# Seven block products for the output projection from the fourth chunk on, and the gate sums in another order

## The chip, the cores and the metric

The kernel runs on one core of a Trainium2 chip. The metric is the device time of one execution in microseconds; lower is better. TensorE (PE) multiplies, VectorE (DVE) and ScalarE (ACT) do the element-wise work and read TensorE's results out of PSUM, GpSimd (POOL) does a little, and SyncE (SP) issues every transfer from one queue, in order.

## The reference

A linear attention feeds a gated feed-forward layer. With batch 8, 8 heads, 576 positions and head size 64:

```
q_s = softmax(q, over head_dim);  k_s = softmax(k, over positions)
kv  = k_s^T v                      (64 x 64 per head)
x   = q_s kv                       -> 4608 tokens x 512
out = ((x @ w_a) * (x @ w_b)) @ w_out      w_a, w_b: 512 x 1536, w_out: 1536 x 512
```

All data is float32. Each operand of a matmul is written as a rounded part and a rest ("hi" and "lo"), and a product is three matmuls: hi by hi, hi by lo, lo by hi.

## The kernel before

The 4608 tokens go in nine chunks of 512 (chunk 0 to chunk 8; the fourth is chunk 3). The 1536 inner columns are twelve blocks of 128 (f), taken as six pairs (i = 0 to 5). Chunk 0 goes a plain way while the weights are still being prepared. From chunk 1 on, one pair of one chunk is a Strassen-Winograd product of a 2 x 2 block matrix of weights (`A11, A12, A22` and the sums `S1` to `S4`) with a 2 x 2 block matrix of x (`B11, B21, B22` and the sums `T1` to `T4`): seven products, each twelve matmuls of 256 columns (`product`, L689), in three PSUM banks (`kx`; `ky`, which is later `kp`; `ka`). Before, the order is A11·B11, S2·T2, S3·T3, S1·T1, A12·B21, S4·B22, A22·T4. ACT copies kx once (L1281), DVE adds the banks into `u2`, `u3` and `cc` (L1282, L1285, L1299, L1312, L1317), and four DVE products of 256 columns turn the sums into the gated values (a times b). `g_split` (L206 on ACT, L209 on DVE) splits two tiles of 512 per pair.

The projection (`project`, L710) takes a gated f, 128 x 512, as the stationary operand in four pieces of 128 tokens and w_out's rows as the moving one: twelve matmuls of 512 columns for each f, into four banks po0 to po3, which collect all twelve f of a chunk. After the last, four copies take them to SBUF (`store`, L723) and four transfers out.

Beside the products of chunk c stands the attention of chunk c + 1, dealt out in pieces by `Spread`: queries (eight exponentials of 64 columns on ACT for each of four head groups, L534), keys, their maximum, and x itself. The weights of each product are loaded from DRAM for each use (`get_w`, L335: 42 transfers of 512 KB in a chunk, eight buffers).

Up to the start of chunk 2 each engine's order is written out by hand (`ORDER`); behind that a scheduler places the instructions, engine by engine, once, when the program is built. Each engine then runs its list in order, and waits where an operand or a buffer is not ready.

## Time and profile before

| | |
|---|---|
| three runs | 959.17, 959.36, 960.6 us |
| profiled execution: first to last instruction (span) | 954.4 us |
| median of the runs less this span | 5.0 us |
| PE busy in the span | 931.9 us (98%) |
| DVE, ACT, POOL busy | 613.4, 390.6, 105.3 us |
| moved by DMA | 282.64 MB, mean 296 GB/s |

The page gives the profiled execution's span and no device time of its own; the 5.0 us between the span and the median lie around it. Busy time is the union of an engine's instructions. Matmuls overlap their neighbours, so what one costs in a dense row is the distance from start to start, not its duration.

### The profile page before, as it was taken

Reading aid. Unit: us, or ns where it says so; the run is one execution under the profiler, and the core shown is the slowest. Engines: PE = TensorE matmul, PEld = TensorE weight load, DVE = VectorE, ACT = ScalarE, POOL = GpSimd, SP = SyncE. Lnnn points to the kernel's source line nnn. Section 1 sums busy time; section 2 is a strip of 40 time slices with the busy share of each in tenths; the row PEclk is TensorE's granted clock in tenths of the full one; section 3 lists DMA queues with packets and bytes.
Section 4 is the critical chain, followed back from the end, with each engine's and each line's share of the span. In section 5 each row is a group of like instructions: output and inputs, shape, how many; then the busy total and the mean of one; then the engine's idle time right before and its main releaser. Section 6 shows DMA issues by size and latency. Waiting matters only on the chain.

```text
span 954.4 us, 17546 instructions
## 1 busy us (share of the span) xinstructions
PE 931.9 (98%) x6479; PEld 827.2 (87%) x6479; DVE 613.4 (64%) x1209; ACT 390.6 (41%) x1085; POOL 105.3 (11%) x88
## 2 busy tenths in 40 slices
PE   5999999999999999999999999999999999999998
PEld 3666667888899999999999999899999999999997
DVE  6979869677676747574756566665756556553443
ACT  7878836523363327141633244323522353121111
POOL 1555352320010001000000000000000000000000
PEclk9999999999999999999999999999999999999999
DMA  9999889898998969896899678976996779677761
GB/s 346 408 413 359 299 286 331 291 324 295 326 374 261 360 226 318 293 393 228 296 296 388 236 275 318 349 269 244 351 332 238 264 272 327 220 258 251 263 211 55
DMA packets 97588, 282.64 MB, mean 296 GB/s; under 512 B 11680, under 2 KB 12256, under 8 KB 97504
## 3 DMA queue, kind: packets, MB, share of 16 engines
q1 hardware_dynamic: 97504, 281.52, 82.9%
q8 instruction: 52, 0.85, 0.4%
q14 instruction: 32, 0.26, 0.1%
HBM read 241.40 MB, written 37.98 MB: 293 GB/s over the span
## 4 chain that ended last, share of the span: by engine, by line
PE 88%; DMA 4%; DVE 4%; ACT 1%; SPq 1%; issue 1%; POOL 0%; POOLq 0%; DVEq 0%; ACTq 0%
PE po L710 27%; PE kx L689 14%; PE kp L689 14%; PE ka L689 14%; PE ky L689 7%; PE pt L664 5%; PE po L699 3%; PE px L620 2%; PE pk L441 2%; DMA mr<-dq 2%; DMA kt_first<-in_kt 1%; DMA ws_y<-dy 1%; DVE ws L209 1%; DMA ws<-dw 1%; DVE wo_w L209 0%
## 5 line engine op out<-in xcount | busy, mean ns | idle before, releaser
L710 PE MATMUL po<-wo_w,gh 128*128 128x512 f32 x768 | 228.1, 396 | 0.0
L689 PE MATMUL kx<-xo,ws 128*128 128x256 f32 x1152 | 164.2, 284 | 0.5 <-ACT u L1281 0.3
L689 PE MATMUL ka<-xo,ws 128*128 128x256 f32 x1152 | 160.8, 282 | 2.1 <-DVE cc L1317 1.0
L710 PEld LDWEIGHTS po<-wo_w,gh 128*128 128x128 f32 x768 | 138.0, 189 | 25.7 <-ACT gh L206 0.3
L689 PE MATMUL kp<-xo,ws 128*128 128x256 f32 x1152 | 157.2, 282 | 0.0
L689 PEld LDWEIGHTS ka<-xo,ws 128*128 128x128 f32 x1152 | 149.7, 188 | 7.1 <-DVE cc L1317 1.2
L689 PEld LDWEIGHTS kx<-xo,ws 128*128 128x128 f32 x1152 | 149.7, 189 | 5.4 <-ACT qt L534 1.0
L689 PEld LDWEIGHTS kp<-xo,ws 128*128 128x128 f32 x1152 | 148.2, 188 | 4.3 <-DVE cc L1299 0.3
L710 PE MATMUL po<-wo_w,gl 128*128 128x512 f32 x384 | 137.7, 396 | 0.0
L206 ACT CAST gh<-cc 128x512 fp32r<-128x512 f32 x96 | 56.7, 620 | 143.9 <-DVE cc L1313 133.3
L1312 DVE TENSOR_TENSOR cc<-kp,u 128x512 f32<-128x512 f32 x48 | 33.1, 689 | 99.6 <-PE kp L689 99.4
L1300 ACT COPY cc<-kx 128x256 f32<-128x256 f32 x48 | 17.9, 373 | 167.0 <-PE kx L689 167.0
L710 PEld LDWEIGHTS po<-wo_w,gl 128*128 128x128 f32 x384 | 71.2, 188 | 15.8 <-DVE gl L209 0.4
L534 ACT ACTIVATE qt<-qt,st 128x64 f32<-128x64 f32 x224 | 75.3, 340 | 22.3 <-DVE st L531 14.3
L664 PE MATMUL pt<-xo,ws 128*128 128x512 f32 x288 | 83.7, 432 | 0.5 <-DVE xo L1048 0.5
L1299 DVE TENSOR_TENSOR cc<-kp,u 128x512 f32<-128x512 f32 x48 | 33.1, 690 | 74.3 <-PE kp L689 74.0
L689 PE MATMUL ky<-xo,ws 128*128 128x256 f32 x576 | 76.9, 282 | 0.8 <-DMA ws<-dw 0.7
L689 PEld LDWEIGHTS ky<-xo,ws 128*128 128x128 f32 x576 | 72.1, 188 | 2.2 <-DVE xf L806 0.9
L209 DVE TENSOR_TENSOR gl<-cc,gh 128x512 fp32r<-128x512 f32 x96 | 63.9, 685 | 13.3 <-ACT gh L206 10.7
L664 PEld LDWEIGHTS pt<-xo,ws 128*128 128x128 f32 x288 | 53.1, 189 | 22.1 <-issue 9.5
L371 POOL PARTITION_ALL_REDUCE mx<-m x20 | 18.4, 918 | 447.2 <-DVE m L382 447.2
L1281 ACT COPY u<-kx 128x512 f32<-128x512 f32 x48 | 28.0, 584 | 82.9 <-PE kx L689 82.0
(147 smaller groups left out, 1148.9 us busy)
## 6 DMA issues: line engine op xcount, KB each, us to landing
ws<-dw SPq DMA_DIRECT2D x312, 512.0 KB, 5.4
dw<-ws SPq DMA_DIRECT2D x42, 512.0 KB, 5.4
mr<-dq SPq DMA_DIRECT2D x112, 128.0 KB, 4.9
raw<-in_w_ab SPq DMA_DIRECT2D x24, 512.0 KB, 7.4
out<-ot SPq DMA_DIRECT2D x36, 256.0 KB, 4.7
vt<-in_v SPq DMA_DIRECT2D x28, 325.0 KB, 6.4
qt<-in_q SPq DMA_DIRECT2D x32, 256.0 KB, 5.2
kt<-in_k SPq DMA_DIRECT2D x24, 320.0 KB, 5.0
```

What stands on the lines that cost most here:

```text
L206: nc.scalar.copy(out=hi, in_=src)
L209: return nc.vector.tensor_tensor(out=lo, in0=src, in1=hi.bitcast(F32), op=ALU.subtract)
L441: nc.tensor.matmul(pk[h * D:(h + 1) * D], kt[:, j, h], vt[:, j, h], start=(j == 0), stop=(j == J - 1),)
L534: nc.scalar.activation(out=qt[:, j, h], in_=qt[:, j, h], func=AF.Exp, bias=st[:, h, 0, j:j + 1], accum_out=st[:, h, 1, j:j + 1],)
L620: nc.tensor.matmul(px[:, s], w, m[:, s], start=(i == 0), stop=(i == 2))
L664: nc.tensor.matmul(pt, w[:, wp], x[g][:, xp], start=(g == 0 and i == 0), stop=(g == NP - 1 and i == 2),)
L689: ins = nc.tensor.matmul(pt[:, n], w[:, n, wp, c], x[:, xp, c], start=(first and n == 0 and i == 0), stop=(i == 5), skip_group_check=True,)
L699: nc.tensor.matmul(po[t], g[:, t * P:(t + 1) * P], wo_first[f], start=(f == 0), stop=(f == NF - 1),)
L710: ins = nc.tensor.matmul(po[t], a[:, ts], wo[f][:, w], start=(f == 0 and i == 0), stop=(f == NF - 1 and i == 2),)
L1281: nc.scalar.copy(out=u2, in_=kx)
L1299: nc.vector.tensor_tensor(out=cc[:, 3], in0=kp, in1=u3, op=ALU.add)
L1312: nc.vector.tensor_tensor(out=cc[:, 1], in0=kp, in1=u2, op=ALU.add)
```

## The change

Chunks 0 to 2 keep their products and their projection. From chunk 3 on three things differ.

1. The projection of a pair is seven block products (`Q1` to `Q7`), each six matmuls of 256 columns: the gated pair is a 2 x 2 block matrix (f by halves of 256 tokens), w_out's two row blocks are another (f by halves of 256 columns). The sums on the left are made by DVE (`left_sums`, four a pair) and each of the seven left operands is split by ACT and DVE (`split_lefts`, 256 columns). The sums on the right are made once (`right_sums`, in chunk 2 and at the start of chunk 3); four of them stay in SBUF for five pairs, the others are stored to DRAM and loaded for each use (`get_right`). Q1, Q5, Q6 and Q7 all accumulate in bank po0; two pairs form a group, and after the last Q1, Q6 and Q7 (or Q5, Q7, Q6) of a group the bank is read out into or added to a tile (`snap`), while the accumulation in the bank goes on.
2. The gate products go in the order A11·B11, S1·T1, S2·T2, A12·B21, S3·T3, A22·T4, S4·B22. A11, S2, S3 and A22 accumulate one after the other in bank kx, and ACT copies the bank after each of the first three (`u3`, `u2`, `u4`; u3 and u4 share a buffer). DVE's adds fall from five to three a pair.
3. Every second chunk takes the pairs backwards, and the seven weights of a chunk's last pair stay for the next chunk's first one. From chunk 4 on the order of PE's products is fixed as written (`chained`). The last pair of chunk 8 is projected as before, at the very end.

```diff
     def get_w(i, op):
+        if (i, op) in last_w:
+            return last_w.pop((i, op))
...
+    def plan(c):
+        groups = [(0, 1), (2, 3), (4, 5)] if c < NCH - 1 else [(0, 1), (2, 3), (4,)]
...
+            text = '4a 1a 2a 6a 3a 7a 5a' if len(ps_) == 1 else '4a 2a 3a 5a 4b 2b 5b 7a 7b 3b 6a 6b 1a 1b' if back else '4a 1a 2a 3a 1b 4b 6a 6b 2b 7a 7b 3b 5a 5b'
...
+    def block_step():
...
+        pt, first = bank(c, {Q2: 1, Q3: 2, Q4: 3}.get(x.m, 0))
...
+        for t in range(2):
+            for n, (ap, wp) in enumerate(((0, 0), (0, 1), (1, 0))):
+                nc.tensor.matmul(pt[:, t], x.left[:, ap, t * P:(t + 1) * P], w[:, wp], ...)
+        if x.snap:
+            n, sign = x.snap
+            with tc.high_priority(100):
+                if sign == 0:
+                    nc.scalar.copy(out=acc_tile(c, n), in_=pt)
+                else:
+                    nc.vector.tensor_tensor(
+                        out=accs[c, n], in0=accs[c, n], in1=pt, op=ALU.subtract if sign < 0 else ALU.add
+                    )
...
+                multiply(kx, A11, B11, True)
+                with pg(100):
+                    nc.scalar.copy(out=u3, in_=kx)
+                block_step()
+                multiply(ky, S1, T1, True)
+                block_step()
+                multiply(kx, S2, T2, False)
+                with pg(100):
+                    nc.scalar.copy(out=u2, in_=kx)
+                block_step()
...
+                multiply(kz, A12, B21, True)
...
+                multiply(kx, S3, T3, False)
+                u4 = sb.tile([P, 2, H], F32, name="u3", bufs=1)
+                with pg(100):
+                    nc.scalar.copy(out=u4, in_=kx)
+                    nc.vector.tensor_tensor(out=cc[:, 3], in0=ky, in1=u4, op=ALU.add)
...
+                if not end:
+                    block_step()
+                    block_step()
...
+                multiply(kx, A22, T4, False)
...
+                last_product = multiply(ky, S4, B22, False)
```

What moves in the engines' lists is shown at three places. In the names, `ws` is a weight, `xo` a split operand (of x, or a right operand that was loaded), `kept` a right operand that stayed, `left` a split left operand, `gh` and `gl` the old split pair, `px` attention of the next chunk.

PE, chunk 3, fourth pair, from its fifth product to its last, before:

```order
L689 MATMUL kx_4704<-xo_3926,ws_4808 128x256 x12
L710 MATMUL po2_4198<-wo5_w_802,gh1_4700 128x512 x2
L710 MATMUL po2_4198<-wo5_w_802,gl1_4701 128x512
L710 MATMUL po3_4199<-wo5_w_802,gh1_4700 128x512 x2
L710 MATMUL po3_4199<-wo5_w_802,gl1_4701 128x512
L620 MATMUL px_4843<-qhl_4782,kvh1_3285 128x256 x2
L620 MATMUL px_4843<-qhl_4782,kvl1_3286 128x256
L620 MATMUL px_4843<-qhl_4782,kvh1_4475 128x256 x2
L620 MATMUL px_4843<-qhl_4782,kvl1_4476 128x256
L689 MATMUL ka_4706<-xo_3933,ws_4871 128x256 x5
L689 MATMUL kp_4793<-xo_3929,ws_4851 128x256 x12
L689 MATMUL ka_4706<-xo_3933,ws_4871 128x256 x7
```

The same pair now, from S2·T2 to its last product; the two kx rows that stand one behind the other are S3·T3 and A22·T4:

```order
L695 MATMUL kx_4906<-xo_3956,ws_4972 128x256 x12
L1403 MATMUL po0_4498<-kept10_3515,left_4414 128x256 x2
L695 MATMUL ka_4908<-xo_4018,ws_5006 128x256 x12
L1403 MATMUL po1_4521<-xo_4329,left_4415 128x256 x6
L1403 MATMUL po0_4498<-kept20_3714,left_4418 128x256 x6
L695 MATMUL kx_4906<-xo_3961,ws_5028 128x256 x12
L695 MATMUL kx_4906<-xo_4025,ws_5073 128x256 x12
L1403 MATMUL po2_4580<-xo_4329,left_4416 128x256 x6
L1403 MATMUL po3_4476<-kept31_3906,left_4414 128x256 x6
L695 MATMUL ky_4907<-xo_4021,ws_5089 128x256 x12
```

Blocks of six stand where runs of 512 columns stood, and one bank is now written by four products with three copies between them.

ACT, chunk 5, in its second pair, between two readings of kx, before (`qt` are the exponentials of the next chunk's queries, `kt` those of its keys):

```order
L1281 COPY u2_6668<-kx_6664 128x512
L206 CAST gh0_6640<-cc_6417 128x512
L206 CAST gh1_6660<-cc_6417 128x512
L534 ACTIVATE qt_6580,st_6420<-qt_6580,st_6420 128x64 x8
L534 ACTIVATE qt_6670,st_6420<-qt_6670,st_6420 128x64 x8
L406 ACTIVATE kt_6683<-kt_6683 128x640
L1300 COPY cc_6667<-kx_6664 128x256
```

And now, from the first to the third copy of kx in that pair:

```order
L1572 COPY u3_7163<-kx_7158 128x512
L540 ACTIVATE qt_7061,st_6903<-qt_7061,st_6903 128x64 x5
L1354 CAST left_4418<-cc_6900 128x256
L1354 CAST left_4419<-cc_6900 128x256
L1354 CAST left_4418<-cc_6900 128x256
L1578 COPY u2_7162<-kx_7158 128x512
L1443 COPY acc_7254<-po0_5958 128x512
L540 ACTIVATE qt_7164,st_6903<-qt_7164,st_6903 128x64 x6
L1354 CAST left_4419<-cc_6900 128x256
L540 ACTIVATE qt_7164,st_6903<-qt_7164,st_6903 128x64 x2
L412 ACTIVATE kt_7177<-kt_7177 128x640
L1594 COPY u3_7332<-kx_7158 128x512
```

The exponentials now lie between copies that the next product in kx needs.

PE, the last rows of the program, before:

```order
L710 MATMUL po0_9977<-wo11_w_1425,gh1_10733 128x512 x2
L710 MATMUL po0_9977<-wo11_w_1425,gl1_10734 128x512
L710 MATMUL po1_9978<-wo11_w_1425,gh1_10733 128x512 x2
L710 MATMUL po1_9978<-wo11_w_1425,gl1_10734 128x512
L710 MATMUL po2_9979<-wo11_w_1425,gh1_10733 128x512 x2
L710 MATMUL po2_9979<-wo11_w_1425,gl1_10734 128x512
L710 MATMUL po3_9980<-wo11_w_1425,gh1_10733 128x512 x2
L710 MATMUL po3_9980<-wo11_w_1425,gl1_10734 128x512
```

And now (`pl` are the banks of the plain last pair):

```order
L1654 MATMUL pl_12017<-xo_11918,xo_11958 128x512 x2
L1654 MATMUL pl_12017<-xo_11918,xo_11959 128x512
L1654 MATMUL pl_12017<-xo_11920,xo_11938 128x512 x2
L1403 MATMUL po0_11197<-kept11_3518,left_4419 128x256 x6
L1654 MATMUL pl_12017<-xo_11920,xo_11939 128x512
L1403 MATMUL po0_11197<-kept10_3515,left_4419 128x256 x6
```

The last two block products, Q7 and Q5 of the fifth pair, stand at the very end, in the bank that is read out between them and after them.

## Rows read from the trace of the kernel before

**Rows 1.** The page: its first line, and part 1's line of busy time (us, share of the span, instructions).

```profile
span 954.4 us, 17546 instructions
...
PE 931.9 (98%) x6479; PEld 827.2 (87%) x6479; DVE 613.4 (64%) x1209; ACT 390.6 (41%) x1085; POOL 105.3 (11%) x88
```

**Rows 2.** Busy time by stretch, about one chunk each: the stretch and its length; busy us (and instructions) of PE, PEld, DVE, ACT, POOL; PE's granted clock; share and rate of the DMA engines.

```profile
240.00:340.00 100.00, 97.91 (x728) 90.71 (x727) 67.78 (x139) 39.01 (x115) 3.45 (x4) 0.98 0.91 322
340.00:440.00 100.00, 100.00 (x760) 93.02 (x759) 63.35 (x132) 36.83 (x111) 3.72 (x4) 1.00 0.83 301
440.00:540.00 100.00, 100.00 (x759) 93.16 (x758) 63.26 (x132) 36.85 (x112) 3.73 (x4) 1.00 0.86 302
...
640.00:740.00 100.00, 100.00 (x753) 93.00 (x753) 62.84 (x131) 36.83 (x111) 3.73 (x4) 1.00 0.83 293
740.00:848.00 108.00, 108.00 (x740) 100.03 (x739) 60.62 (x115) 37.81 (x114) 0.00 (x0) 1.00 0.79 269
848.00:954.00 106.00, 102.59 (x699) 94.19 (x697) 42.55 (x74) 16.75 (x32) 0.00 (x0) 1.00 0.59 203
```

**Rows 3.** Everything that PE waited for from 345 us to the end: us in total, times, longest.

```profile
PE ky L689 <- DMA ws<-dw: 0.7, 1, 0.7
```

**Rows 4.** PE in order of time in chunk 4: start, duration, what. Two gate products of twelve matmuls, the first and the last of a run of twelve projection matmuls (three, one, one, one, two, one, two, one), and the product behind it.

```profile
524.11 1.60 PE L689 MATMUL ky<-xo,ws 128*128 128x256 f32 x12
525.55 1.60 PE L689 MATMUL ka<-xo,ws 128*128 128x256 f32 x12
526.99 0.86 PE L710 MATMUL po<-wo_w,gh 128*128 128x512 f32 x3
...
529.56 0.39 PE L710 MATMUL po<-wo_w,gl 128*128 128x512 f32 x1
529.79 1.35 PE L689 MATMUL kx<-xo,ws 128*128 128x256 f32 x10
```

**Rows 5.** Groups of equal instructions with their shapes: count, busy us and mean ns, idle time before them and what ended it. DVE's subtraction and ACT's cast of a split, DVE's add from PSUM, ACT's copies of a bank and of half a bank, DVE's product and its subtraction at 256 columns.

```profile
L209 DVE TENSOR_TENSOR gl<-cc,gh 128x512 fp32r<-128x512 f32 x96 | 63.9, 685 | 13.3 <-ACT gh L206 10.7 <-PE po L710 2.7
L206 ACT CAST gh<-cc 128x512 fp32r<-128x512 f32 x96 | 56.7, 620 | 143.9 <-DVE cc L1313 133.3 <-PE ky L689 5.6 <-DVE cc L1318 3.1
L1299 DVE TENSOR_TENSOR cc<-kp,u 128x512 f32<-128x512 f32 x48 | 33.1, 690 | 74.3 <-PE kp L689 74.0
...
L1281 ACT COPY u<-kx 128x512 f32<-128x512 f32 x48 | 28.0, 584 | 82.9 <-PE kx L689 82.0 <-DVE st L538 0.9
...
L1300 ACT COPY cc<-kx 128x256 f32<-128x256 f32 x48 | 17.9, 373 | 167.0 <-PE kx L689 167.0
...
L209 DVE TENSOR_TENSOR kvl<-kv,kvh 128x256 fp32r<-128x256 f32 x10 | 4.2, 421 | 0.2
```

**Rows 6.** All engines in order of time in chunk 5: four DVE instructions in a row, and the end of a product in kx with ACT's copy of it.

```profile
586.49 0.69 DVE L1312 TENSOR_TENSOR cc<-kp,u 128x512 f32<-128x512 f32 x1 [1.02 <-PE kp L689]
...
587.09 0.68 DVE L1317 TENSOR_TENSOR cc<-ka,u 128x512 f32<-128x512 f32 x1
587.69 0.42 DVE L1313 TENSOR_TENSOR cc<-cc 128x256 f32<-128x256 f32 x1
...
588.02 0.42 DVE L1318 TENSOR_TENSOR cc<-cc 128x256 f32<-128x256 f32 x1
...
589.11 0.50 PE L689 MATMUL kx<-xo,ws 128*128 128x256 f32 x2
...
589.45 1.58 PE L689 MATMUL ky<-xo,ws 128*128 128x256 f32 x12
589.65 0.59 ACT L1281 COPY u<-kx 128x512 f32<-128x512 f32 x1 [0.37 <-PE kx L689]
```

**Rows 7.** ACT in order of time in chunk 5: the second and the last of eight exponentials of queries in a row, and one of keys.

```profile
560.05 0.33 ACT L534 ACTIVATE qt<-qt,st 128x64 f32<-128x64 f32 x1
...
562.04 0.33 ACT L534 ACTIVATE qt<-qt,st 128x64 f32<-128x64 f32 x1
...
562.48 0.74 ACT L406 ACTIVATE kt<-kt 128x640 f32<-128x640 f32 x1
```

**Rows 8.** Transfers from 340 to 440 us: GB/s in 40 slices, the amount, and a weight's load with KB each and median us from issue to landing.

```profile
GB/s 313 380 354 8 310 110 206 356 365 161 273 295 364 296 319 383 410 406 417 269 337 191 205 185 212 374 382 411 412 403 417 416 415 391 340 293 220 82 336 23
DMA packets 10306, 30.10 MB, mean 301 GB/s; under 512 B 1264, under 2 KB 1328, under 8 KB 10297
...
ws<-dw SPq DMA_DIRECT2D x42, 512.0 KB, 5.9
```

**Rows 9.** The last 11 us in order of time: the last split's cast, the two matmuls that waited for the split, the last matmul and the last copy.

```profile
943.81 1.24 ACT L206 CAST gh<-cc 128x512 fp32r<-128x512 f32 x2 [8.64 <-DVE cc L1313]
...
944.48 0.74 PE L710 MATMUL po<-wo_w,gh 128*128 128x512 f32 x2
945.21 0.19 PEld L710 LDWEIGHTS po<-wo_w,gl 128*128 128x128 f32 x1 [0.43 <-DVE gl L209]
...
950.20 0.40 PE L710 MATMUL po<-wo_w,gl 128*128 128x512 f32 x1
950.63 0.59 ACT L723 COPY ot<-po 128x512 f32<-128x512 f32 x1 [0.81 <-PE po L710]
```

**Rows 10.** The smallest transfer from the list of all transfers: KB and us from issue to landing.

```profile
ident<-in_eye SPq DMA_DIRECT2D x1, 64.0 KB, 2.0
```

More of the change, by code (lines that the diff above doesn't have):

```diff
@@ L1315, in linear_attention_then_gated_ffn @@
[L1315 to L1320 removed]
+                if c == BY_BLOCKS - 1 and p > 0:
+                    right_sums(p - 1)
+                if po is None and not blocks_of:
+                    po = [ps.tile([P, DM], F32, name=f"po{t}") for t in range(TT)]
```

364 lines of the change are left out of this document (317 added, 47 removed).

## The prediction

> **What bounds the kernel now.** The page's busy times come first: PE works 931.9 of the span's 954.4 us, DVE 613.4, ACT 390.6 [rows 1]. The windows of one chunk each show that this is no mere average: from 340 to 740 us PE is busy in every microsecond, at a granted clock of 1.00, the 2.4 GHz level; DVE has 63 of 100 us, ACT 37, and the DMA engines 0.83 to 0.86 of their time [rows 2]. Third, PE's waits: from 345 us to the end the list gives one wait of 0.7 us [rows 3]. So PE's columns set the time, and each microsecond less on PE counts as long as no other engine hands its part over late. The base of the sum is the profiled execution: span 954.4 + 5.0 around it = 959.4 us, beside a median of 959.36.
>
> **PE, the gain.** What a matmul costs in a dense row is read from start to start. Twelve gate matmuls of 256 columns take 525.55 - 524.11 = 1.44 us, 0.12 each; twelve projection matmuls of 512 columns take 529.79 - 526.99 = 2.80 us, 0.2333 each [rows 4]. The projection of a pair was 24 of the latter, 5.60 us; it becomes 7 x 6 = 42 of 256 columns, in the shape of the gate products, 42 x 0.12 = 5.04 us. The gate products stay 84 a pair in either order. That is 0.56 us a pair, and 6 chunks x 6 pairs less the last, plain one make 35 pairs: **-19.6 us**.
>
> The Trainium skill (TensorE: Matmul & The Clock Gate, "Wait — 56ns, not 53.3ns?") gives N / 2.4 GHz + about 2.5 ns a matmul, as an estimate 109 and 216 ns here, so 35 x 0.59 = 20.7 us. The rows show 120 and 233 ns; they decide, and 19.6 stays.
>
> **DVE and ACT, the load.** In a dense stretch DVE starts a 512-column instruction every 0.60 us and a 256-column one every 0.34 [rows 6], less than their durations of 0.685 and 0.421 [rows 5]. A pair was 5 adds + 2 splits of 512 columns and 4 products of 256: 7 x 0.60 + 4 x 0.34 = 5.56 us. Now it is 3 adds of 512, and 4 products, 4 left sums and 7 split rests of 256: 3 x 0.60 + 15 x 0.34 = 6.90. Six snaps and five final sums of 512 come to each chunk, 6.6 us. Together 6 x 1.34 + 6.6 = +14.7 us, from 63 to some 77 of 96 us a chunk. ACT had a copy of a bank (0.584), one of half a bank (0.373) and two casts (0.620) a pair [rows 5], with pitches a little below these some 2.1 us; now three copies and seven casts of 256 columns. For such a cast, not in the rows, I take 0.30 us, half of 0.620, between nothing and the 0.373 of the half bank: 3.8 us. With the stores' copies replaced by three snaps and one copy that is +10 to +12 us, from 37 to about 48 of 96. Both have room on average: no term by itself, unless a single stretch is full.
>
> **Hand-overs in kx.** The bank is now written by A11, S2, S3 and A22, with a copy of ACT after each of the first three. What PE must wait if nothing stood between two of them is read from chunk 5: the next product starts at 589.45, 0.16 before the old one's last group ends at 589.61; ACT starts at 589.65 (+0.04) and takes 0.59 [rows 6]; a matmul starts 0.05 after what it waited for, as at the end, where the first of two casts is over at 943.81 + 0.62 = 944.43 and its matmul starts at 944.48 [rows 9]. So 0.16 + 0.04 + 0.59 + 0.05 = 0.84 us. One block product (0.72 us) hides all but 0.12, two (1.44 us) all of it. In the fixed order two blocks, or a product of 1.44 us, stand at each place, so from chunk 4 on I cost these copies at nothing where ACT is free; the cover is gone where ACT is busy or the order differs:
>
> - *Chunk 3*, ordered by the scheduler. The change's first list shows A22·T4 directly behind S3·T3 in its fourth pair; the second and sixth go the same way: 3 x 0.84 = 2.5. One pair with a single block before A12 and one with two snaps close together add 1.5: **+4.0** (0 to 6).
> - *The second pair of chunks 4 to 7.* From the first pair's A12 add to the second's, DVE has 11 instructions of 512 and 17 of 256 columns: 6.6 + 5.8 = 12.4 us, and the attention's, of which a chunk has 63 - 6 x 5.56 = 30 us, a sixth 5 [rows 2, 6]: 17.4 us of work in a PE period of 96.2 / 6 = 16.0. If DVE comes late, u4 (in u3's buffer) cannot be copied, and A22 waits on PE. ACT's list agrees: between the copies to u2 and u4 now stand eight exponentials at 0.33 from start to start (2.66 us), a copy, a cast, and one of keys of 0.74 [rows 7]: 4.2 us, where PE has some 6 us of work. The full 1.4 us excess is one bound, with slack left from the pair before 0 the other, 2.5 with a late ACT too. I take 1.0 a chunk: **+4.0** (0 to 10).
>
> **The end.** The last pair of chunk 8 is plain and S3, A22 stand with no block between: 0.84. The last two blocks, Q7 and Q5, use one bank that DVE reads between them: 0.16 + 0.04 + 0.69 [rows 5] + 0.05, less one 512-column matmul between (0.23) = 0.70. Before, PE waited 0.29 + 0.43 here for the split [rows 9]; the plain pair still does. After the last matmul came a copy and a store of 256 KB, to the span's end 954.4 - 950.6 = 3.8 us [rows 9]. Now a copy (0.6), an add (0.6), and three or four half-bank sums (1.4) precede the store of a half (128 KB; between 2.0 for 64 KB [rows 10] and 3.2, I take 2.6): 5.3 less 3.8 is 1.5 more, less what can overlap. Sum **+2.3** (0 to 4).
>
> **Transfers.** Chunk 2 stores right operands, 6.0 MB, chunk 3 loads 22 x 256 KB and stores 0.75 MB, later chunks load 5.8 MB of them and save 7 x 512 KB = 3.7 MB of weights. The densest slices move 415 GB/s [rows 8], so these cost 14.5, 15.7 and 5 us of the engines' time. On shares of 0.91, 0.83 and 0.83 to 0.86 [rows 2] chunk 2 gets to 105 us of work in 100, chunk 3 to 98 in 96, later chunks to 88 in 96. Eight buffers hold a lead of 8 x 2 = 16 us over a landing of 5.9 [rows 8], so a short excess is borrowed from it. I take **+1** (0 to 7).
>
> Sum: 959.4 - 19.6 + 4.0 + 4.0 + 2.3 + 1.0 = **951.1 us**, own range 946 to 956.
>
> **The rivals.**
>
> *A. All cover holds.* Neither chunk 3 nor the second pairs stall: 959.4 - 19.6 + 2.3 = 942 (941 to 946). For it: DVE at 77 and ACT at 48 of 96, and slack that carries over. Against it: the two bare neighbours in chunk 3's list, which no other engine can cover. Chance 0.20.
>
> *B. The one-bank hand-overs show in every pair; slower.* The same 0.84 us, or a snap in po0 (four of the seven blocks write it), comes out each time because ACT reaches its copy late behind exponentials and casts in its list. From (19.6 - 2.3) / 35 = 0.49 us a pair nothing is gained; at 0.84 it is 959.4 - 19.6 + 2.3 + 29.4 = 971.5 us. For it: ACT's list above and a bank count that leaves kx one bank. Against it: 1.44 us of other matmuls stand in the gap in chunks 4 to 8, and ACT's average load is half. Chance 0.14. This is the side on which the Trainium skill stands (Perfetto Trace Analysis, "Matmuls"): independent matmul groups should rotate through different banks so that reading one overlaps the next group, and larger matmuls are more efficient than small ones. Rows 4 bear out its second half, 0.120 against 2 x 0.1167 for double the columns, 3%; the first no row before can show.
>
> *C. Transfers bind in chunks 2 and 3.* PE waits for weights or right operands for the whole excess, 7 us in place of 1, and some stay behind later: 951 + 7 = 958 (956 to 961). For it: 105 us in 100. Against it: PE's only wait for a weight was 0.7 us [rows 3], at shares of 0.83 to 0.91. Chance 0.11.
>
> *D. The columns are not saved.* A block's matmul would take 0.133 us or more, and 42 cost the old 5.60; with the 11 us of losses 970. The gate products have just this shape at 0.120 [rows 4]. Chance 0.02.
>
> **How the numbers follow.** My forecast has 0.53, A 0.20, B 0.14, C 0.11, D 0.02. 0.2%, 1.9 us, is about what a measurement of this kernel can tell from no change, so faster means below 957.4: forecast, A, and 0.05 of C give 0.78; same is the rest of C, 0.06; slower, over 961.3, is B and D, 0.16. The range must leave out at most 0.20: B and D above (0.16) and the lowest part of A (0.04). That gives 942 to 960.
>
> **What would show it.** Starts of block matmuls 0.12 us apart, 35 x 42 = 1,470 of them; a chunk from the fifth on takes about 96 to 97 us where it took 99.6; DVE has some 77 us of it and ACT 48. PE's waits from chunk 3 on, one line before, should name the kx copies of u2 and u4 and snaps, some 10 us in all, concentrated in chunk 3 and the second pairs; below 4 us A is right, above 17 us, spread over all pairs, B, and waits for weights or right operands of over 5 us C. At the end PE should stop about 5 us before the span does. The forecast is wrong if DVE's pitch in the new small instructions is well above 0.34 us (at 0.42, 35 x 15 x 0.08 = 42 us more work fill its slack and every pair stalls), or if the waits in kx are paid in no list that I read.

## The result, and the profile after

The changed kernel takes 968.17 us in the median (963.97 to 970.25, 7 runs); the kernel before takes 959.36 (956.47 to 961.8, 7 runs beside it). The ratio is 1.0076, 95% interval 1.0051 to 1.0101: about 7 us slower, where 8 us faster had been forecast and 942 to 960 given as the range.

The page of the changed kernel, first line and busy times, answers to [rows 1]:

```profile
span 966.1 us, 19712 instructions
...
PE 920.6 (95%) x7109; PEld 846.4 (88%) x7109; DVE 722.1 (75%) x1572; ACT 484.4 (50%) x1346; POOL 102.9 (11%) x88
```

PE's work fell by 11.3 us, but it is no longer dense. The windows, with the columns of [rows 2], show where:

```profile
240.00:340.00 100.00, 95.67 (x704) 87.31 (x703) 77.91 (x163) 41.64 (x119) 3.25 (x4) 1.00 0.98 351
340.00:440.00 100.00, 95.57 (x797) 91.30 (x796) 75.17 (x173) 50.15 (x147) 3.26 (x4) 1.00 0.99 361
440.00:540.00 100.00, 95.95 (x837) 93.59 (x837) 77.37 (x184) 51.34 (x154) 3.52 (x4) 1.00 0.92 303
...
640.00:740.00 100.00, 98.25 (x861) 96.39 (x860) 76.93 (x183) 51.23 (x153) 4.12 (x4) 1.00 0.95 316
740.00:848.00 108.00, 105.53 (x874) 104.46 (x873) 79.88 (x178) 52.20 (x159) 0.00 (x0) 1.00 0.90 316
```

From 340 us on every window of PE has a hole of 2 to 4 us where there was none, at a granted clock of 1.00 as before. DVE's 77 and ACT's 51 us are near the forecast (77 and 48 of 96). The DMA engines are busy 0.98 and 0.99 of the two windows that hold most of chunks 2 and 3, and 0.90 to 0.95 of the later ones, near what the sum had given (88 of 96). PE's longest waits from 345 us to the end, which had been one line of 0.7 us [rows 3]; the whole list adds up to 14.8:

```profile
PE kx L695 <- ACT u L1594: 4.6, 6, 1.5
PE kx L695 <- DMA ws<-dw: 2.8, 2, 1.7
PE px L626 <- DVE xf L812: 2.0, 2, 1.1
PE kx L695 <- ACT u L1578: 1.4, 1, 1.4
PE pk L447 <- DVE sst L553: 1.0, 2, 0.6
```

L1594 is the copy to u4 behind S3·T3, the one that A22·T4 needs. The bare hand-over stands in chunk 3 as the order had shown it; here in its sixth pair, PE in order of time (start, duration, and in brackets the idle time before it):

```profile
455.97 1.58 PE L695 MATMUL kx<-xo,ws 128*128 128x256 f32 x12
458.27 1.70 PE L695 MATMUL kx<-xo,ws 128*128 128x256 f32 x12 [0.73 <-ACT u L1594]
```

From start to start 2.30 us pass where twelve matmuls take 1.43: 0.87 us for a forecast 0.84. (The 0.73 in the brackets is counted from the modelled end of the last matmul, and so is less.)

The longest u4 wait has another cause. All engines in chunk 4, in its fourth pair:

```profile
518.76 3.89 SPq L581 DMA_DIRECT2D mr<-dq  x4
...
523.39 0.69 DVE L587 TENSOR_TENSOR qtt<-qtt,mr 128x512 f32<-128x512 f32 x1 [3.73 <-DMA mr<-dq]
...
524.00 0.68 DVE L1587 TENSOR_TENSOR cc<-ka,u 128x512 f32<-128x512 f32 x1
...
524.77 0.58 ACT L1594 COPY u<-kx 128x512 f32<-128x512 f32 x1
...
525.41 1.68 PE L695 MATMUL kx<-xo,ws 128*128 128x256 f32 x12 [1.48 <-ACT u L1594]
```

`mr` are rows of the next chunk's softmax (maxima and denominators), stored to DRAM (`dq`) and loaded back spread over 64 partitions, 16 transfers of 128 KB a chunk. They land late, DVE stands for 3.73 us at the instruction that needs them, the gate sum L1587 stands behind it, u4 shares the buffer that L1587 frees, and A22 waits on PE. Summed from 355 to 960 us, DVE's waits for these rows are, in the kernel before and in the changed one (line, releaser: us, times, longest):

```profile
DVE qtt L581 <- DMA mr<-dq: 1.7, 1, 1.7
```

```profile
DVE qtt L587 <- DMA mr<-dq: 15.3, 8, 4.0
```

The issues of transfers from 459 to 855 us show it too, the rows most of all: KB each and median us from issue to landing, changed kernel first, the kernel before (its second profile, e4 below) behind it.

```profile
ws<-dw SPq DMA_DIRECT2D x140, 512.0 KB, 6.7
mr<-dq SPq DMA_DIRECT2D x64, 128.0 KB, 7.8
dq<-sst SPq DMA_DIRECT2D x4, 32.0 KB, 6.2
```

```profile
ws<-dw SPq DMA_DIRECT2D x168, 512.0 KB, 5.2
mr<-dq SPq DMA_DIRECT2D x64, 128.0 KB, 4.7
dq<-sst SPq DMA_DIRECT2D x4, 32.0 KB, 2.2
```

The end, which answers to [rows 9]: Q7's accumulation is read, Q5 waits for it, and after the last matmuls (958.21 on) DVE has a row of sums.

```profile
957.47 0.69 DVE L1415 TENSOR_TENSOR acc<-acc,po 128x512 f32<-128x512 f32 x1 [2.78 <-PE po L1403]
...
958.21 0.98 PE L1403 MATMUL po<-kept,left 128*128 128x256 f32 x6 [0.55 <-DVE acc L1415]
...
959.23 0.58 ACT L1443 COPY acc<-po 128x512 f32<-128x512 f32 x1 [8.98 <-PE po L1403]
...
961.50 1.42 DVE L1661 TENSOR_TENSOR acc<-pl,acc 128x256 f32<-128x256 f32 x4
```

**By chunk.** A chunk is taken from the first matmul of its first product to the next chunk's (504 product matmuls each), chunk 8 to the span's end. "Columns" is what its matmuls take at the pitches of their shapes (0.119 and 0.232 us for 256 and 512 columns), the rest are waits and, in chunk 8, the end behind the last matmul. Lengths in us, of one profile each; e1, e3, e7 and e13 are experiments below.

| chunk | before (e4) | columns | after | columns | e1 | e3 | e7 | e13 |
|---|---|---|---|---|---|---|---|---|
| 1 | 110.5 | 98.6 | 110.3 | 98.5 | 110.7 | 110.4 | 110.0 | 113.2 |
| 2 | 104.2 | 99.7 | 106.6 | 99.6 | 104.6 | 108.6 | 105.0 | 105.4 |
| 3 | 99.4 | 98.6 | 102.2 | 93.6 | 97.9 | 105.7 | 97.5 | 102.3 |
| 4 | 99.6 | 98.9 | 101.8 | 95.4 | 99.8 | 94.7 | 98.4 | 98.4 |
| 5 | 99.9 | 99.2 | 100.7 | 95.8 | 98.6 | 101.5 | 98.1 | 99.5 |
| 6 | 100.2 | 99.5 | 100.7 | 96.1 | 98.9 | 98.2 | 97.4 | 98.8 |
| 7 | 96.4 | 96.2 | 95.5 | 92.8 | 95.5 | 94.6 | 93.2 | 92.6 |
| 8 | 103.2 | 98.7 | 106.2 | 97.5 | 106.5 | 104.1 | 104.5 | 106.2 |

The columns of chunks 3 to 8 add to 591.1 before and 571.2 after: 19.9 us were saved, as forecast (19.6). The lengths of these chunks, less columns and less the end behind the last matmul's start (4.2 us before, 7.2 after), leave 3.4 us of waits before and 28.7 after. So waits took back 25.3 us, the end 3.0, and chunk 2 another 2.4.

### The profile page after: what moved, and what is told of

The parts are those of the page before. It is cut to its first block, busy times and chain, and to the rows that moved or that the text cites. A ratio compares the mean times of both kernels' runs of the same rounds, so it can differ in the third digit from the quotient of the medians.

```text
span 966.1 us, 19712 instructions
## 1 busy us (share of the span) xinstructions
PE 920.6 (95%) x7109; PEld 846.4 (88%) x7109; DVE 722.1 (75%) x1572; ACT 484.4 (50%) x1346; POOL 102.9 (11%) x88
## 4 chain that ended last, share of the span: by engine, by line
PE 71%; DMA 16%; DVE 6%; SPq 3%; ACT 2%; issue 1%; DVEq 0%; ACTq 0%
PE kx L695 19%; PE po L1403 13%; PE ky L695 10%; PE pt L670 7%; PE ka L695 6%; DMA ws<-dw 6%; PE po L716 5%; PE po L705 4%; DMA xo<-dr 2%; PE kp L695 2%; DMA kt<-in_k 2%; PE pk L447 2%; DMA mr<-dq 2%; DMA qtt<-in_q_late 2%; SPq L581 2%; PE px L626 1%
## 5 line engine op out<-in xcount | busy, mean ns | idle before, releaser
L695 PE MATMUL kx<-xo,ws 128*128 128x256 f32 x2016 | 272.1, 284 | 12.4 <-ACT u L1594 4.6
L695 PEld LDWEIGHTS kx<-xo,ws 128*128 128x128 f32 x2016 | 252.2, 188 | 19.4 <-ACT u L1594 6.0
L1354 ACT CAST left<-cc 128x256 fp32r<-128x256 f32 x245 | 93.3, 405 | 112.6 <-DVE cc L1588 33.2
L1355 DVE TENSOR_TENSOR left<-cc,left 128x256 fp32r<-128x256 f32 x245 | 97.7, 419 | 29.4 <-ACT left L1354 28.9
L1403 PE MATMUL po<-kept,left 128*128 128x256 f32 x720 | 106.4, 283 | 1.4 <-DVE left L1355 0.9
L1403 PE MATMUL po<-xo,left 128*128 128x256 f32 x750 | 106.7, 282 | 0.2 <-DVE acc L1415 0.2
L695 PE MATMUL ka<-xo,ws 128*128 128x256 f32 x720 | 97.0, 282 | 1.9 <-DMA ws<-dw 1.1
L1403 PEld LDWEIGHTS po<-xo,left 128*128 128x128 f32 x750 | 96.6, 189 | 0.6 <-DVE acc L1415 0.4
L1403 PEld LDWEIGHTS po<-kept,left 128*128 128x128 f32 x720 | 94.5, 189 | 2.4 <-DVE left L1355 1.1
L716 PE MATMUL po<-wo_w,gh 128*128 128x512 f32 x192 | 55.3, 398 | 0.6 <-ACT gh L208 0.6
L1587 DVE TENSOR_TENSOR cc<-ka,u 128x512 f32<-128x512 f32 x36 | 24.8, 689 | 33.8 <-PE ka L695 33.3
```

Source lines behind the costliest of these rows:

```text
L695: ins = nc.tensor.matmul(pt[:, n], w[:, n, wp, c], x[:, xp, c], start=(first and n == 0 and i == 0), stop=(i == 5), skip_group_check=True,)
L716: ins = nc.tensor.matmul(po[t], a[:, ts], wo[f][:, w], start=(f == 0 and i == 0), stop=(f == NF - 1 and i == 2),)
L1354: nc.scalar.copy(out=a[:, 0], in_=cc[:, n, part])
L1355: nc.vector.tensor_tensor(out=a[:, 1], in0=cc[:, n, part], in1=a[:, 0].bitcast(F32), op=ALU.subtract)
L1403: nc.tensor.matmul(pt[:, t], x.left[:, ap, t * P:(t + 1) * P], w[:, wp], start=(first and t == 0 and n == 0), stop=(n == 2), skip_group_ch ...
L1587: nc.vector.tensor_tensor(out=cc[:, 0], in0=kz, in1=u3, op=ALU.add)
```

## The experiments

Each was run beside the kernel before on the same chip; ratios are to it, and at 959 us 0.001 is about 1 us. The changed kernel's ratio is 1.0076. An edit does more than its lines say: the scheduler places every program anew, and in chunk 3 nothing holds PE's order. In the changed kernel S3·T3 and A22·T4 stand bare, one behind the other, in three pairs of chunk 3; so they do in e13, but in e1 and e6 in one pair only. And one profile is no exact measure of a chunk: in e11 all engines have the same instructions in the same order as the changed kernel from chunk 3 to 7, and yet its chunks 4 to 7 are 5.3 us shorter (393.4 for 398.7).

**e1: the loads of right operands left out** (changed kernel).

```diff
         w = moved[x] = held["ring"][n % 4 // 2][:, n % 2]
-        nc.sync.dma_start(out=w.bitcast(F32), in_=d_right[x.i, x.m])
+        if n < 4:
+            nc.sync.dma_start(out=w.bitcast(F32), in_=d_right[x.i, x.m])
```

> Leaves out all loads of right operands after the first four (121 of 125 transfers of 256 KB); the block products read whatever lies in the ring, so only the time counts. Theory T (transfers): the new loads keep the transfer engines at 0.93 to 0.98 of their time, other loads land late, and DVE, ACT and PE wait for them in their order; then this kernel is 6 us or more below the changed one (under 962), and PE's waits for weights (6 us in the profile of after) and the late u4 copies of the fourth pairs go. Theory H (hand-overs and order): the loss is PE's waits for copies of kx, the cut-up keys' products and the longer end, which no load causes; then it stays within 3 us of the changed kernel (965 to 970).

Measured: 957.29 us, ratio 0.9992 (0.9964 to 1.0020). Leaving out the loads wins 0.0084, some 8 us (4 to 12 by the two intervals), as the first theory had it, and PE waits for no weight from 345 us on. But of the 10.0 us that chunks 3 to 8 get shorter in the profiles 4.3 lie in chunk 3, where two of the three bare hand-overs go with the new placing. And the rows stay late: DVE waits 10.2 us for them (15.3), and they land in a median 7.5 us (7.8), so their lateness is not the loads' doing alone. Without the loads the kernel is still no faster than before: as much again went elsewhere.

**e2: the new order of the gate products alone**, in the kernel before (old projection, no chain).

```diff
+            if c < 3:
                 multiply(kx, A11, B11, True)
...
+            else:
+                kz = ka
+                multiply(kx, A11, B11, True)
...
+                multiply(ky, S1, T1, True)
+                multiply(kx, S2, T2, False)
...
```

> The kernel before with the new order of the gate products and their adds from chunk 3 on, the old projection, all else old. Theory H: the one-bank order costs PE a wait for a copy of kx in many pairs, some 0.1 to 0.2 us a pair and more beside the attention: 962 to 968. Theory T: DVE and ACT have less to do and no transfer is added, so it is within 2 us of the kernel before (957 to 961).

Measured: 973.73 us, ratio 1.0163 (1.0119 to 1.0206), more than either theory gave. PE waits from 355 us on:

```profile
PE ka L689 <- DMA ws<-dw: 5.1, 7, 2.0
PE kx L689 <- DMA ws<-dw: 2.1, 3, 1.0
PE kx L689 <- DVE cc L1359: 1.8, 1, 1.8
PE kx L689 <- ACT u L1343: 1.7, 5, 0.7
...
PE kx L689 <- ACT u L1330: 0.7, 1, 0.7
```

No transfer was added here, and yet weights come late. So the order is a loss by itself, if the scheduler is to place it; only a part of it is the copies of kx. Why the weights are late here is not shown. The keys' products still stand in 8 runs of 40.

**e3: the block products alone**, in the old order of the gate products, without the fixed order.

```diff
-            held["chain"] = (c, p) >= (4, 0)
+            held["chain"] = False
...
-            if c < BY_BLOCKS:
+            if True:
                 multiply(kx, A11, B11, True)
...
```

> The changed kernel with the old order of the gate products (banks kx, ky, ka in turn, five adds a pair) and PE's order left to the scheduler in all chunks; block products, right operands and the reversed turns stay. Theory T: the loads are all there, so it is no better than 964. Theory H: the hand-overs of kx are gone and the keys' products stand together, so most of the 19.6 us of saved columns shows: 950 to 957, less what the busier DVE takes.

Measured: 958.65 us, ratio 1.0002 (0.9982 to 1.0022), between the two forecasts: 7 us better than the changed kernel and level with the one before. In this run DVE waits for no row at all from 355 us on, with the same loads. Chunks 4 and 7 show what the blocks give (94.7 and 94.6 us), chunks 2 and 3 take 10.7 back.

The longest of PE's waits in chunk 3 costs more than its own 4.0 us. DVE is held up by the attention's work in its list, and behind the wait TensorE's granted clock is at the lower of its two levels (1.2 GHz for 2.4). Two rows of PE, and the window from 402.0 to 405.4 us with its granted clock of 0.51:

```profile
401.32 2.37 PE L695 MATMUL kp<-xo,ws 128*128 128x256 f32 x12 [4.00 <-DVE u L1512]
403.49 1.48 PE L1403 MATMUL po<-xo,left 128*128 128x256 f32 x6
402.00:405.40 3.40, 3.40 (x18) 3.40 (x17) 1.97 (x5) 0.97 (x2) 0.00 (x0) 0.51 0.80 274
```

From start to start the twelve take 2.17 us instead of 1.43.

**e4: the kernel before once more.**

> The kernel before once more, for a second profile of it. Both theories: ratio 1.000 with an interval of about 0.002 on either side; if its profile is of a run near 959 us, the places where it is longer than the first profile (a run of some 956.4) show what of the 4 us that chunks 1 and 2 seem to have lost is a difference between runs.

Measured: 958.59 us, ratio 1.0005 (0.9981 to 1.0028). Its profiled run took 956.46 with a span of 954.7, so 1.8 us lie around a span, not the 5.0 that I had put in: by that, the profile of before was of a run some 3 us faster than the median. Its chunk 1 is 110.5 us (108.3 in the first profile), with PE waiting 2.6 for weights; in the profiles of all kernels here chunk 1 takes from 108.3 to 113.5 us.

**e5: the attention's matmuls in the fixed order too** (changed kernel).

```diff
+                begin = len(traced)
                 for now in self.todo[:want]:
                     for s in now:
                         s()
+                if held.get("chain"):
+                    chained.extend(x for x in traced[begin:] if x.engine == mybir.EngineType.PE)
```

> The changed kernel with the attention's matmuls put into the fixed order of PE too, where they are written: from chunk 4 on the 40 matmuls of a pair of keys' products stand together again (8 runs where 22 were from 340 us on). Theory K (cut-up keys): each extra run of them costs PE some 0.35 us (22 runs took 19.2 us, before 8 took 12.0), and with it go 4 to 6 us: 962 to 964. Theory D (late DVE and ACT, through transfers and the second pairs' load): the cut pieces only fill time in which PE would wait anyway, and it stays within 2 us of the changed kernel (966 to 970), with longer waits for u4.

Measured: 996.45 us, ratio 1.0389 (1.0361 to 1.0418). PE's longest waits from 459 to 890 us:

```profile
PE pst L551 <- DVE st L545: 18.4, 4, 4.9
PE po L1406 <- DMA xo<-dr: 4.4, 4, 1.4
```

Keys' products stand together, and PE pays with a wait of 4.6 us a chunk for the softmax sums. So theory K fails as a cure: where they are written, the attention's results are not ready. What a cut-up run costs is not tested by it.

**e6: the right operands' loads with a quarter of the bytes.**

```diff
-        nc.sync.dma_start(out=w.bitcast(F32), in_=d_right[x.i, x.m])
+        part = P if n < 4 else 32
+        nc.sync.dma_start(out=w.bitcast(F32)[0:part], in_=d_right[x.i, x.m][0:part])
```

> The changed kernel with as many transfers of right operands as now, each with a quarter of its bytes from the fifth on (32 of 128 partitions, 64 KB); the rest of an operand is whatever lies in the ring, so only the time counts. If the bytes are what costs (theory B), it is within 3 us of the kernel without the loads (957 to 960). If the number of issues and their place in SP's queue are what costs (theory Q: each waits in the one queue for its ring slot, and weights stand behind), it stays at 964 to 969.

Measured: 965.59 us, ratio 1.0067 (1.0040 to 1.0094). Three quarters of the bytes are gone, and by the ratio 0.0009 is won, within intervals that allow up to 4 us. So the bytes are not shown to be what the loads cost, nor ruled out as a part of it. The profiled run, the fastest of five (962.54 us), has chunks 3 to 8 4.5 us shorter than the changed kernel's, but 2.7 of it in chunk 3, where two bare hand-overs go as in e1.

**e7: e3 without the loads** (the edit of e1 in e3).

> Block products with the old order of the gate products (as e3) and no loads of right operands after the first four (as e1); the operands are wrong, only the time counts. If loads and the new order are the two losses and add up, it is some 10 us below e3 and e1 both: 946 to 951. If DVE's extra work is a loss of its own (77 of 96 us), it stays above 953, with PE's waits for DVE in many pairs.

Measured: 953.36 us, ratio 0.9933 (0.9914 to 0.9952), the only one clearly below the kernel before, though by 6.4 us and not by the 19.6 of its columns, and above the 946 to 951 expected. The other reading, DVE's work as a loss of its own, lacks its sign: from 345 us on PE waits 4.9 us in all, 2.9 of it for DVE, in a few places and not in many pairs. Against e3 the loads cost 0.0069, 6.6 us (4 to 9); against e1 the new order with its chain costs 0.0059, 5.7 us (2 to 9), where no load is in the way. So in a table of two by two, loads and order each cost about as much with the other as without. The ten runs go with the granted clock: 947.95 us, the profiled one, at a mean of 0.999; 949.71 and 950.36 at 0.997; 954.11 and 956.25 at 0.992.

**e8: the fixed order from the third pair of chunk 3.**

```diff
-            held["chain"] = (c, p) >= (4, 0)
+            held["chain"] = (c, p) >= (3, 2)
```

> The changed kernel with the fixed order of gate and block products from the third pair of chunk 3 on instead of from chunk 4. Theory H for chunk 3: the two bare hand-overs of S3 to A22 there (0.89 us each) and what stands around them go: 1.5 to 3 us less, 965 to 966.5. Rival: the scheduler had put them so because something else was late; then chunk 3 stays at 102 us.

Measured: 969.20 us, ratio 1.0103 (1.0078 to 1.0128). Neither forecast came: chunk 3 is longer, 105.2 us. Two of the three u4 waits go, and waits for the attention come in their place (px 2.9, pst 1.2).

**e9: the right operands' loads in POOL's queue.**

```diff
-        nc.sync.dma_start(out=w.bitcast(F32), in_=d_right[x.i, x.m])
+        nc.gpsimd.dma_start(out=w.bitcast(F32), in_=d_right[x.i, x.m])
```

> The changed kernel with the right operands' loads issued by POOL, in a queue of their own, instead of SP; same bytes, same ring. Theory Q (SP's one queue): the loads wait there for a slot of the ring (64.8 us of SP's time from 355 to 850 us in the profile of after), and weights, queries and broadcast rows stand behind them and land late; then most of the 11 us that the loads cost goes: 957 to 962. Theory B (bytes and busy transfer engines): the bytes are the same, so 965 to 970. If POOL's own issuing is slow, its blocks wait and it is above 970.

Measured: 978.17 us, ratio 1.0208 (1.0174 to 1.0242), some 13 us more than the changed kernel. DVE still waits 15.9 us for rows, so in this run SP's waiting for the ring is not what makes them late. It is no clean test, since POOL itself now waits (456 us for PE in front of these issues), with the keys' maxima behind.

**e10: e3 with the loads in POOL's queue.**

> Block products with the old order of the gate products (as e3), the loads of right operands in POOL's queue (as e9). Theory Q: near the kernel without those loads (e7, 953.4): 951 to 956, faster than the kernel before. Theory B: as e3, 957 to 960.

Measured: 962.90 us, ratio 1.0043 (1.0024 to 1.0063): above both forecasts, and worse than e3 by 4 us.

**e11: the last blocks ahead of the plain pair.**

```diff
-    behind_each_other(chained)
     for engine, names in ORDER.items():
...
                         )
+                        chained.append(ins.ins)
...
+    behind_each_other(chained)
```

> The changed kernel with the last block products ahead of the plain pair's matmuls on PE, in a fixed order; nothing else. From the last matmul's start to the span's end 7.2 us pass in after (4.2 before), and Q7 to Q5 has a wait of 0.71. Both theories: the snap, the copy and the sums of the last group come under the plain pair's matmuls (11 us), so the end takes 4 to 4.5 us and the wait goes: 2.5 to 3.7 us less than after, 964.5 to 966. If DVE's order at the end is what counts, the end stays over 6 us.

Measured: 967.36 us, ratio 1.0104 (1.0039 to 1.0168), too wide to tell by the time. The profile, of a run of 960.34 us, tells: from the last matmul's start to the end 4.1 us (7.2), while the blocks' own waits for snaps rise from 0.71 to 1.75; chunk 8 is 1.9 us shorter.

**e12: e3 with the end of e11.**

> Block products with the old order of the gate products (as e3) and the last block products ahead of the plain pair's matmuls (as e11). In e3 6.3 us lie between the last matmul's start and the span's end, in e11 4.1. If the end is a loss of its own, it is 2 to 2.5 us below e3 in the same terms: ratio 0.997 to 0.999, 956 to 958. If the last group's sums only move their wait to the front of the plain pair, it stays at 1.000.

Measured: 959.34 us, ratio 0.9992 (0.9978 to 1.0007): with e3 at 1.0002, a gain of 1 us, within the intervals. Level with the kernel before.

**e13: the rows loaded once and used again.**

```diff
+    rows_kept = {}
...
-                box["r"] = q_rows(c, g, every["dq"])
+                if c < 5:
+                    box["r"] = rows_kept[g] = q_rows(c, g, every["dq"])
+                else:
+                    box["r"] = rows_kept[g]
```

> The changed kernel in which the broadcast rows of the queries (16 transfers of 128 KB a chunk) are loaded for chunks 3 and 4 alone and used again in all later ones, which leaves out their loads from chunk 5's on; the values are wrong, only the time counts. Theory M (late rows): DVE's waits for them (15 us in after) go, and with them the stalls of PE in the fourth pairs: 4 to 7 us less than after, 961 to 964. Theory B (bytes): 2 MB a chunk less, by the 2.6 us that e6 gave for 4.3 MB some 1 us: 966 to 968.

Measured: 960.06 us, ratio 1.0010 (1.0000 to 1.0020): 6.3 us less than the changed kernel (4 to 9), for 2 MB a chunk, while e6 got no clear gain for 4.3 MB. All that PE waited for from 459 to 855 us is then

```profile
PE kx L695 <- ACT u L1599: 0.9, 2, 0.7
PE pk L447 <- DVE sst L553: 0.6, 1, 0.6
PE pk L447 <- issue: 0.4, 1, 0.4
```

No wait for a weight is left either, though all loads are there, and chunk 7 takes 92.6 us, what its columns take (92.8). Theory M held: in chunks 4 to 7 PE's listed waits are 8.6 us in the changed kernel, 3.8 without the loads (e1) and 1.2 without the rows. There rows and loads cost together, in the stretch in which the rows go through SP's list. The edit takes away the rows' 64 transfers from 459 to 855 us, their bytes and DVE's standing for them at once, and does not say which counts.

**e14: the rows first in SP's list.**

```diff
...
-                nc.sync.dma_start(
...
+                with tc.high_priority(300 if roomy(c) else 0):
+                    nc.sync.dma_start(
...
```

> The changed kernel with a higher priority for the broadcast rows and for the store they read, so that in SP's list all 16 stand together where the first stood, ahead of the weights and right operands that stood among them; all bytes stay. Theory M: DVE's waits for the rows fall from 15 to under 5 us, and the kernel gains 2 to 5 us on after: 963 to 966. If the weights behind them come late instead, PE's waits for weights rise by as much: 967 to 970.

Measured: 966.82 us, ratio 1.0089 (1.0063 to 1.0114): no gain. DVE waits for no row any more, but PE waits for what stands behind them (459 to 855 us):

```profile
PE ky L697 <- DMA ws<-dw: 5.7, 2, 3.4
PE pst L551 <- DVE st L545: 1.6, 1, 1.6
PE po L1405 <- DMA xo<-dr: 1.3, 2, 0.9
```

By this profile the lateness is moved, not removed. It is of the slowest of four runs (972.37 us; the other three took 965.09 to 967.26), and behind its waits of 3.41 and 2.28 us for weights the granted clock falls to 0.50 from 518.4 and from 723.2 us.

**e15: e14 with the end of e11.**

> The rows first (as e14) and the last block products ahead of the plain pair (as e11). If the two losses are separate, their gains add: 960 to 964, at best even with the kernel before. If it is no better than e14, the end costs nothing by itself.

Measured: 965.23 us, ratio 1.0067 (1.0043 to 1.0091); 2 us better than e14, within the intervals.

**e16 and e17: the rows in half as many transfers**, in the changed kernel and in e12.

```diff
...
+                    nc.sync.dma_start(
+                        out=rows[w],
+                        in_=dq[g, :, w].unsqueeze(1).broadcast_to([2, D, T]),
+                    )
...
```

> The changed kernel with the broadcast rows of chunks 4 to 8 in 8 transfers of 256 KB where there were 16 of 128 KB, same bytes and values. Theory N (number in flight): SP's waits for landings fall from 90 us to some 60 and DVE's waits for rows from 15 to under 8; the kernel gains 2 to 5 us on after: 963 to 966. Theory B (bytes): no gain over 1 us, 967 to 969.

> Block products in the old order of the gate products, the last blocks ahead of the plain pair (as e12), and the rows merged (as e16). Theory N: the waits for weights and right operands in the fourth pairs (some 3 us in e12) shrink: 955 to 958, ratio 0.996 to 0.998, faster than the kernel before. Theory B: as e12, 0.999 to 1.000.

Measured: 1125.26 and 1118.99 us, ratios 1.1738 (1.1705 to 1.1771) and 1.1673 (1.1644 to 1.1701). Each chunk with such rows takes some 30 us more. Transfers from 459 to 855 us, GB/s in 40 slices:

```profile
GB/s 258 336 286 183 293 396 407 253 96 49 94 200 233 378 359 125 164 344 386 403 372 116 97 51 139 279 260 392 300 106 241 323 389 380 145 49 94 94 262 275
```

Two or three slices of a chunk, of 10 us each, move 49 to 97 GB/s, while PE waits up to 16.4 us for the load of a right operand. One such stretch, in the columns of [rows 2]:

```profile
550.00:560.00 10.00, 2.00 (x9) 2.00 (x10) 2.44 (x6) 2.67 (x7) 0.00 (x0) 0.57 0.13 49
```

The DMA engines are busy 0.13 of the time, the work of about two of the sixteen, so they are not full; a transfer of this form is slow, and the loads behind it come late. Part of the 30 us is the clock: behind the waits it stands at 0.50 for up to 30.7 us at a stretch (from 438.8 us). On the number of transfers the two say nothing.

**e18: one transfer of 512 KB for two of the right operands.**

```diff
-        nc.sync.dma_start(out=w.bitcast(F32), in_=d_right[x.i, x.m])
+        if n < 4:
+            nc.sync.dma_start(out=w.bitcast(F32), in_=d_right[x.i, x.m])
+        elif n % 2 == 1:
+            two = held["ring"][n % 4 // 2].bitcast(F32)
+            nc.sync.dma_start(out=two.rearrange("p a b c -> p (a b c)"), in_=d_right[0, "whole"].rearrange("p a b -> p (a b)"))
```

> The changed kernel with one transfer of 512 KB for every two of 256 KB of the right operands, from the fifth on; it fills the same ring with other data, so only the time counts. Same bytes, half the number, in packets of 4 KB where they were 2 KB. Theory N: about half of what leaving them out gave (11 us): 961 to 965, SP's waits for landings under 65 us. Theory B: within 2 us of after (966 to 970), less what the larger packets save (some 1 us).

Measured: 972.59 us, ratio 1.0148 (1.0120 to 1.0176), worse by 7 us. Half the number does not help; each transfer now needs two free slots of the ring, and SP's longest wait for PE in front of one is 6.8 us. Theory N fails in this form.

## Why the prediction was wrong

**What held.** The pitch of a block matmul (0.119) and the 19.6 us of columns (19.9). The bare hand-over (0.84 us forecast, 0.87 to 0.89), Q7 to Q5 (0.70, measured 0.71). Chunk 3's hand-overs (4.0 forecast; u4 2.7 and u2 1.6 there). DVE's load. ACT's is a little more than worked out, because a cast of 256 columns takes 0.405 us and not the 0.30 that I had taken, which is above even the bound of 0.373:

```profile
L1354 ACT CAST left<-cc 128x256 fp32r<-128x256 f32 x245 | 93.3, 405 | 112.6 <-DVE cc L1588 33.2
```

**What came out near for another reason.** For the second pairs of chunks 4 to 7 I had forecast 1.0 us each, as A22 waiting for a late copy to u4. About their fifth product the list names 0.56, 0.22, 0.47 and 0.73 us. But only the 0.22, in chunk 5, is A22 behind that copy. In chunks 4 and 6 a keys' product waits for DVE's copy of the softmax sums (L553), and in chunk 7 the transposes of these sums (pst) wait for the copy; there DVE had stood 1.5 us for a query's load. The size is partly luck.

**The step that failed** is the transfers' term: "so a short excess is borrowed from it. I take **+1** (0 to 7)". The loads cost 8 us (e1 against the changed kernel, 4 to 12; 6.6 in the old order, e7 against e3), where I had taken 1; that is above the upper bound of 7 too, though by less than the intervals can tell. I had added bytes at the rate of the densest slices and looked at the weights' lead. What I left out is what else goes through SP's list: the softmax rows, which go out to DRAM and come back, and for which DVE stands in front of the gate sums. In the changed kernel DVE waits 15.3 us for them, and in chunks 4 to 7 PE's listed waits fall from 8.6 us to 1.2 without the rows (e13, all loads in place) and to 3.8 without the loads (e1, all rows in place). So there the price is rows and loads together. The rows had no place in the sum. It is not the whole of the loads' price: in the old order DVE waits for no row (e3), and yet the loads cost 6.6; in the two profiles most of it, 8.2, lies in chunk 3 (e3 less e7), where PE's order differs between the two. Rival C, with 7 us in chunks 2 and 3, was the nearest in size; but its sign, over 5 us of waits for weights or right operands, did not come (2.8).

**The second failure** is a term that the sum did not have: what the fixed order does to the attention's matmuls. "From chunk 4 on I cost these copies at nothing where ACT is free" looks at the copies alone. The new order with its chain costs 5.7 us without any loads (e1 against e7), no more than the 8.0 that I had put in for hand-overs, but it is made up otherwise. Around fixed products the attention falls into the gaps that are left. The keys' products stood in 8 runs of 40 from 340 us on, now in 22. In the kernel before, and in the changed one:

```profile
567.80 1.39 PE L441 MATMUL pk<-vt,kt 128*64 128x65 f32 x40
569.12 1.57 PE L689 MATMUL kp<-xo,ws 128*128 128x256 f32 x11
```

```profile
575.42 0.33 PE L447 MATMUL pk<-vt,kt 128*64 128x65 f32 x2
575.67 1.57 PE L695 MATMUL kx<-xo,ws 128*128 128x256 f32 x11
```

From the start of the matmul before a run to the start of the one behind it, less the 0.119 us of the former, a run of 40 takes 1.41 us and one of two 0.35. All runs together take 11.3 us before and 16.5 in the changed kernel, with 1.0 of waits for the softmax sums in it: 5.2 us that stand nowhere in the sum. Between e7 (12 runs) and e1 (20) they go from 12.2 to 16.5. The rows point to the chain rather than the order as what cuts them: chunk 3, in the new order without the chain, holds them in 3 runs, the chained chunks 4 to 6 in 5, 8 and 6; and e2, the order without blocks or chain, leaves them whole. In e13 chunks 4 to 6 still hold 2.7 to 3.7 us beyond their columns, where the kernel before has 0.7; keys' runs and the waits in front of them are most of the difference. On the Trainium skill's rule (Perfetto Trace Analysis, "Matmuls": rotate independent groups through banks), the trace agrees where two products stand bare, 0.87 us each, as far as the rule applies: these products add up in one bank and are independent only in what is read between them. But that is a small part of what the order costs, and e2, where PE's listed waits for copies are 2.4 us in all, loses 15.6.

**The smaller ones.** After the last matmul the end took 3.0 us more, for 1.5: DVE's sums do not overlap, they stand in one row. Chunk 2, for which only the transfers' term spoke, grew by 2.4 us in these two profiles; in those of e1, e5, e6, e8, e9, e11, e13 and e14, which share it, it takes 104.4 to 106.6 us, 104.2 and 104.7 before, so about 1 us is the change's. And the 5.0 us around the span were 2, the rest a difference between runs: against profiles alone the miss is 966.1 for 946.1.

**The sum.** In profiles, before (e4) to after: -19.9 columns, +25.3 waits in chunks 3 to 8, +3.0 at the end, +2.4 in chunk 2 and +0.5 ahead of it give +11.3; the spans differ by 11.4. Of the waits some 10 go with the loads (e1's chunks 3 to 8 are that much shorter, the new placing of chunk 3 included), and 5.2 are the longer keys' runs.

**What stays open.** How a load of 256 KB hurts is not shown. Its bytes (e6) won nothing clear, half its number (e18) won nothing, though each transfer then needs two slots, and taking it out of SP's list (e9) did not bring the rows in time, though that run put POOL in the way. DVE's waits for the rows follow neither the loads nor the order alone: 15.3 us in the new order with the loads and 10.2 without (e1), 0 in the old order with the loads (e3) and 7.3 without (e7). So the order in which SP issues them, dq's store and weights between them, may have a part; e14, which changed that order, won nothing clear. What each edit owes to the scheduler's new placing was not taken apart. The granted clock has a share that no experiment takes apart: the block kernels' runs show a mean of 0.995 (changed kernel, e3, e7, medians), the kernel before 0.998, which over 960 us is some 3 us, as an estimate for a PE that is dense; in the profiled run of the changed kernel the clock was 1.00 in all windows shown, and the loss stands there without it. No version with all its work beat the kernel before: the best, e12, is level with it.

## What to carry to other kernels

Saved columns count only as long as PE stays dense: before a dense engine is relieved by 2%, every list that feeds it has to be checked at its fullest stretch, not on average. A new stream of loads is priced together with what shares its queue; look first at round trips through DRAM whose reader sits in an in-order engine ahead of critical work. An order that fixes the main products leaves the side work only the gaps, in pieces, and each piece has a price of its own. And where a scheduler places the program, an experiment that leaves something out also moves the rest: compare the orders before the time is put down to what was left out.

## What the runs showed of the hardware

- SP never had more than eight transfers in flight, in the whole of the profiles of before, e4, after, e3 and e13; in the changed kernel's its transfers signal on eight semaphores in turn. Worked out from issue and landing of each transfer from 459 to 855 us: 66 of 300 issues before found seven others in flight, 215 of 357 in the changed kernel, 62 of 299 in e13; none found more. SP's waits for landings of earlier transfers add up to 19 us before (e4), 90 after and 18 in e13; in e3, where no row is late, they are 72. Three of the lines after:

```profile
SPq L341 <- DMA ws<-dw: 25.8, 28, 2.2
SPq L581 <- DMA ws<-dw: 15.9, 13, 2.1
SPq L1338 <- DMA ws<-dw: 14.0, 15, 2.4
```

- A load whose source repeats two rows over 64 partitions each in one transfer (e16) brought whole stretches down to 49 to 97 GB/s, at 0.13 of the DMA engines' time, about two of the sixteen, where the same bytes in two transfers did not.
- Two matmuls of 65 columns on half the array's width between full ones cost 0.35 us, 40 of them 1.41, so 38 more cost 1.06: most of a short run is the change into it and out.
- Behind PE's waits of 4.0 us (e3, e12), 3.41 and 2.28 us (e14) and 1.98 us (e6) the granted clock stood at 0.50, its lower level, though PE was at work again; twelve matmuls took 2.17 us instead of 1.43 (e3). Behind waits of 2.05 us (e3) and 2.69 us (e8) it stayed at 1.00.
